# The order of the w1 side's units in the Strassen groups of a SwiGLU's first pair: its third product ahead of its fourth, and the second products spread between them

## The chip, the cores and the metric

One core of one Trainium2 chip runs the program. The metric is the device time of one execution in microseconds (us), as the median of several runs. The profile is of one further execution of the same kernel, with a time of its own.

## The reference

An FNet block (a Fourier mixing of the sequence) and a SwiGLU block, each behind a layer norm whose scale and shift come from a condition vector c. S = 2048 positions, D = 512 features, F = 1792 hidden features, all fp32. Cut to what matters:

```python
mod = (_silu(c) @ w_mod).reshape(1, 6, 1, -1)
sa, ca, ga, sb, cb, gb = (mod[:, i] for i in range(6))
h = _layernorm(x) * (1 + ca) + sa
a = einsum("bsd,ed->bse", h, dft_hid_re); b = einsum("bsd,ed->bse", h, dft_hid_im)
x = x + ga * (einsum("ts,bse->bte", dft_seq_re, a) - einsum("ts,bse->bte", dft_seq_im, b))
h = _layernorm(x) * (1 + cb) + sb
gate, up = h @ w1, h @ w3
x = x + gb * ((_silu(gate) * up) @ w2)
```

The change lies in the last two lines, the SwiGLU.

## The kernel before

**Numbers.** Every fp32 operand is held as two tiles, a high part and a low part (names ending in h and l), and every product is made of three matmuls: high by high, low by high, high by low. So w1h and w1l are the parts of a block of w1, h2h and h2l of the normed input, and hf holds both parts of the hidden tile silu(gate) * up.

**Tiling.** The sequence lies in four tiles t of 512 positions, the hidden features in seven blocks g of 256. The tiles form two pairs, (0, 2) and (1, 3). For a block and a pair, the products with w1 and with w3 are done by Strassen's scheme: seven products where eight would be due, with sums of quarters of the weight (w1s, w3s and their parts w1sh, w1sl, w3sh, w3sl) and sums of input tiles (th, tl). One such (block, pair) is a group. `items` lists twelve groups, `i` counts them: i = 0 to 4 are the blocks 2 to 6 of the first pair, i = 5 to 11 those of the second.

**Units.** A group's work on TensorE (PE) is a list of units of six matmuls each: a1 to a7 are the seven products with w1, b1 to b7 those with w3, and y is one *second product*, a piece of the product with w2 of the group before; eight of these are due in a group. The main loop at lines 1799 to 1825 has the order as a string. For i = 1 to 4 it is a head, `-b7 a1 a2 -b4 -b3` (the minus marks the last w3 units of the group before), and then `body`; i = 0 has the head `a1 a2`. Other groups have strings of their own, so `body` as the diff has it holds for i = 0 to 4 alone. Here y1 to y5 are the second products in `body`, in their order.

**PSUM banks.** The seven products of a side are accumulated in three banks (`TO`, line 1222): products 1, 6, 7 and 4 go one after the other on top of one another into the side's first bank (0 for w1, 3 for w3), product 2 into the second, products 5 and 3 into the third. Between two of them the bank's content is read out, in `factor` (lines 1361 to 1407):

- after 1, 6 and 5, ScalarE (ACT) copies the bank to a tile x or y (`copy`, L87);
- after 7, 2 and 3, VectorE (DVE) adds such a tile to the bank (`plus`, L93), into v for w1 and in place for w3;
- after 4 the bank is used itself, for w1 by the silu on ACT (L1244), for w3 by a multiplication on DVE (L96).

So a7 can't start before ACT has copied what a6 left, and a4 can't start before DVE has added what a7 left; for w3 b7 waits for the copy after b6, and b4 for the addition after b7 in the same way. a3 waits for the copy of what a5 left in its own bank, and for nothing of a7 or a4. Each y takes bank 6 or 7 in turn and is read out by ACT (L335), or by DVE in four units of i = 0 (L1153, its y2 to y5); a second product thus waits for the reading out of the second product two before. Every two of them are added to a sum in HBM by a DMA that GpSimd (POOL) issues (L1160).

**After the w3 units.** The tile v (silu(gate) times up) is copied to hf's high part on ACT one unit later and its low part is made on DVE another unit later (`behind`, `result`, L87 and L90). The y units of the next group read hf.

**Other work in the same queues.** Each engine works its own queue in order. After each unit `beside` (line 1690) puts more work on DVE and ACT, by credits: first what is in `jobs`, the splitting of the next weights (`weight_jobs`, lines 1178 to 1212: w1h, w1s, w1l, w1sh, w1sl and the same for w3, `w2h` and `w2l` for w2); and only when `jobs` is empty, the `background`: the second layer norm of tiles 1 and 3 (`ln2`, line 818: t, L826, L828, L838, L840, a square root on ACT at L880 that needs another activation table, its reciprocal L883, L847, L848, xc at L96 and L894). The jobs of the next group's w1 are queued at a3, those of its w3 at b3, those of w2 at b2.

A second kernel for other input (`general`) lies behind a branch and isn't executed.

Of the kernel before, what the change touches and what calls it, by code (L numbers as in the profile page):

```python
# [42 lines left out]
def folded(nc, pools, c, cp, wmr, wmc, x, xt, ctr, cti, wdr, wdi, w1, w3, w2, out):  # L43
# [1659 lines left out]
    def down(g, pair, *which):  # L1703
        key = which[-1]
        drain(lambda: (key, "l") in done, jobs)
        delayed()
        if (g, pair) in SEVEN:
            seven_unit(g, pair, *which)
        else:
            down_unit(g, pair, *which)  # L1710
        beside(1.36, USED["own" if pair == 1 and g >= NG - 2 else "y"])
# [85 lines left out]
    ln2(1)  # L1797
    ln2(3)
    for i in range(len(items)):
        body = "a6 a5 y a7 y y a4 y a3 y b1 y b2 y b6 b5 y"  # L1800
        if i and items[i - 1] in SEVEN:
            body = "a6 a5 a7 y a3 a4 y b1 b2 y b6 b5 y"
        spread = i > 1 and items[i - 2] in SEVEN
        if spread and i < len(items) - 1:
            body = body.replace("a6", "a6 y", 1)
        if i == len(items) - 2:
            body = "a6 y a5 y a7 a3 y a4 b1 y b2 b6 y b5"
        if i == turning:
            body = "y y y y y a6 y a5 y a7 y b1 b2 a4 b6 a3 b5"
        if i == len(items) - 1:  # L1810
            body = "a6 a5 a7 a3 a4 b1 b2 y b6 y b5 y b7 y b4 y y b3 y y y y y y y y y y"
        head = "-b7 a1 -b4 -b3 a2 " if i == turning else "-b7 a1 a2 -b4 -b3 " if i else "a1 a2 "
        if spread and i < len(items) - 1:
            head = "-b7 a1 y a2 -b4 y -b3 "
        if i == len(items) - 1:
            head = "-b7 y a1 a2 y -b4 y -b3 "
        for at in (head + body).split():
            if at == "y":
                if (i, len(seconds)) == (len(items) - 1, 4):
                    tc.mark_branch_hint_location("general", hint="LikelyTaken")  # L1820
                down(*seconds.popleft())
            elif at[0] == "-":
                unit(at[1], i - 1, int(at[2]))
            else:
                unit(at[0], i, int(at[1]))
# [710 lines left out]
def fnet_swiglu_block(  # L2536
# [26 lines left out]
    pools = consts, small, big, psum  # L2563
    args = c, cp, wmr, wmc, x, xt, ctr, cti, wdr, wdi, w1, w3, w2, out
    bad = folded(nc, (*pools, dram, tc), *args)
    flag = nc.values_load(
        bad[0:1, 0:1],
# [62 lines left out]
```

## Time and profile before

| | |
|---|---|
| median of 3 runs | 700.3 us (699.35 to 700.66) |
| profiled execution | 698.81 us, its span from first to last instruction 697.0 us |
| mean granted TensorE clock | 0.996 |
| busy PE / DVE / ACT / POOL | 97% / 84% / 65% / 19% of the span |
| groups i = 0 to 4 | about 317.5 to 475 us of the span |

The profile's page gives each engine's busy time, the granted clock in 40 slices, and the chain of work that ended last. A row of the timeline has the start in us, the busy time of one instruction or of a run of equal ones, the engine, the line, the operation, output and inputs by the program's names, and in brackets the idle time ahead of it with what ended that. Matmuls are pipelined, so the row's busy time is longer than their spacing: it is the starts of two rows that tell how far apart they were.

### The profile page before, as it was taken

How to read it: one execution, taken by the hardware profiler on the slowest of the kernel's cores; microseconds unless marked ns; L12 is line 12 of the kernel's file. 1: busy time of each engine (PE TensorE's matmuls, PEld its weight loads, DVE VectorE, ACT ScalarE, POOL GpSimd, SP SyncE). 2: the span in 40 equal slices, each digit the busy share in tenths (PEclk: the TensorE clock that was granted, in tenths of full speed). 3: DMA queues.
4: the chain of work that ended last, by engine and by line, in shares of the span. 5: the costliest groups of instructions: out<-in, count | busy, mean ns of one | idle time of the engine just before them, and what ended most of it. 6: DMA issues, size and time to landing. Idle time of an engine off the chain costs nothing.

```text
span 697.0 us, 9026 instructions
## 1 busy us (share of the span) xinstructions
PE 677.9 (97%) x3122; PEld 557.1 (80%) x3122; DVE 587.9 (84%) x945; ACT 451.4 (65%) x751; POOL 133.6 (19%) x156
## 2 busy tenths in 40 slices
PE   7999899999999999999999999999999999999996
PEld 5898778888888888888877788787877888888785
DVE  5999779987999977989987886898899979888373
ACT  4998965455343665664566767677676978777620
POOL 1320253543445000100100001011002221121100
PEclk9999999999999999999999999999999999999999
DMA  8730299787578431363758566456939898999703
GB/s 265 217 122 1 74 329 364 254 291 243 186 287 294 152 140 31 63 119 121 133 114 166 132 151 124 88 94 144 265 87 200 150 221 163 187 212 170 186 39 125
DMA packets 40261, 116.80 MB, mean 168 GB/s; under 512 B 5136, under 2 KB 5392, under 8 KB 40208
## 3 DMA queue, kind: packets, MB, share of 16 engines
q0 software_dynamic: 14512, 50.86, 35.8%
q1 hardware_dynamic: 25264, 63.98, 27.6%
q10 hardware_dynamic: 432, 1.31, 0.6%
q8 instruction: 26, 0.43, 0.3%
q14 instruction: 27, 0.22, 0.1%
HBM read 76.81 MB, written 41.42 MB: 170 GB/s over the span
## 4 chain that ended last, share of the span: by engine, by line
PE 73%; DVE 11%; ACT 8%; issue 3%; DMA 3%; SPq 1%; another core or an unknown queue 1%; POOL 0%; ACTq 0%; POOLq 0%
PE bank L100 45%; PE bank L750 25%; PE bank L559 1%; DMA wmr<-in_wmr 1%; ACT y L335 1%; DMA sum<-y 1%; ACT hf L87 1%; DVE v L96 1%; PE bank L598 1%; DVE xc L96 1%; SPq L231 1%; ACT xc L894 1%; DVE x L93 1%; DVE w3s L90 1%; DVE v L93 1%
## 5 line engine op out<-in xcount | busy, mean ns | idle before, releaser
L100 PE MATMUL bank<-hf,w2h 128*128 128x512 f32 (+1 forms) x352 | 108.8, 390 | 0.5 <-ACT y L335 0.4
L87 ACT ACTIVATE hf<-v 128x512 fp32r<-128x512 f32 x71 | 44.3, 630 | 64.6 <-DVE v L96 53.8
L335 ACT ACTIVATE y<-bank,gb 128x512 f32<-128x512 f32 x118 | 76.5, 682 | 5.2 <-PE bank L100 5.1
L100 PEld LDWEIGHTS bank<-hf,w2h 128*128 128x128 f32 x352 | 65.4, 188 | 16.9 <-ACT y L335 2.2
L1160 POOL DMA_DIRECT2D sum<-y x28 | 24.0, 857 | 245.1 <-ACT y L335 125.1
L100 PE MATMUL bank<-hf,w2l 128*128 128x512 f32 (+1 forms) x176 | 68.1, 387 | 0.0
L90 DVE TENSOR_TENSOR hf<-v,hf 128x512 fp32r<-128x512 f32 x71 | 48.8, 687 | 13.8 <-ACT hf L87 13.8
L1352 POOL DMA_DIRECT2D sum<-y x35 | 29.8, 852 | 129.3 <-ACT y L335 124.9
L750 PE MATMUL bank<-d,us 128*128 128x512 f32 x128 | 49.9, 390 | 1.0 <-DVE ho L93 1.0
L750 PE MATMUL bank<-bh,us 128*128 128x512 f32 x128 | 49.9, 390 | 0.0
L750 PE MATMUL bank<-bh,ul 128*128 128x512 f32 x128 | 49.8, 389 | 0.0
L750 PE MATMUL bank<-d,uh 128*128 128x512 f32 x128 | 49.8, 389 | 0.0
L750 PE MATMUL bank<-l,us 128*128 128x512 f32 x128 | 49.8, 389 | 0.0
L750 PE MATMUL bank<-l,uh 128*128 128x512 f32 x128 | 49.8, 389 | 0.0
L170 POOL DMA_INDIRECT re<-in_ctr,mirror x32 | 37.2, 1162 | 65.6 <-DVE ul L90 38.5
L87 ACT ACTIVATE x<-bank 128x512 f32<-128x512 f32 x72 | 41.5, 591 | 11.9 <-PE bank L100 11.8
L170 POOL DMA_INDIRECT im<-in_cti,mirror x32 | 32.8, 1025 | 36.6 <-PE bank L750 11.6
L100 PEld LDWEIGHTS bank<-hf,w2l 128*128 128x128 f32 x176 | 33.0, 188 | 6.7
L93 DVE TENSOR_TENSOR v<-bank,x 128x512 f32<-128x512 f32 x36 | 24.7, 687 | 15.9 <-PE bank L100 14.8
L1244 ACT ACTIVATE v<-v 128x512 f32<-128x512 f32 x36 | 22.7, 630 | 23.2 <-DVE v L93 22.8
L93 DVE TENSOR_TENSOR x<-bank,x 128x512 f32<-128x512 f32 x36 | 24.6, 685 | 9.4 <-PE bank L100 9.1
L100 PE MATMUL bank<-h2h,w1h 128*128 128x512 f32 x80 | 31.1, 389 | 0.0
(260 smaller groups left out, 1906.3 us busy)
## 6 DMA issues: line engine op xcount, KB each, us to landing
sum<-y POOLq DMA_DIRECT2D x63, 512.0 KB
w<-in_w SPq DMA_DIRECT2D x42, 512.0 KB
re<-in_ctr SPq DMA_DIRECT2D x32, 256.0 KB
im<-in_cti SPq DMA_DIRECT2D x32, 256.0 KB
wmc<-in_wmc SPq DMA_DIRECT2D x8, 512.0 KB
xr<-in_xt SPq DMA_DIRECT2D x8, 512.0 KB
sum<-xr SPq DMA_DIRECT2D x8, 512.0 KB
x<-in_x SPq DMA_DIRECT2D x11, 256.0 KB
```

The lines of the kernel that those rows point to most:

```text
L87: nc.scalar.activation(dst, src, AF.Copy, scale=scale)
L90: nc.vector.tensor_tensor(out=dst, in0=a, in1=b, op=OP.subtract)
L93: nc.vector.tensor_tensor(out=dst, in0=a, in1=b, op=OP.add)
L96: nc.vector.tensor_tensor(out=dst, in0=a, in1=b, op=OP.mult)
L100: nc.tensor.matmul(acc, lhs[a], rhs[b], start=first and n == 0, stop=last and n == len(PASSES) - 1, skip_group_check=more,)
L170: nc.gpsimd.indirect_dma_start(dst, None, rows, bass.IndirectOffsetOnAxis(ap=at, axis=0))
L231: queue.dma_start(raw_w[dt][q * 64 : (q + 1) * 64, m, :], w[i][par::2, q])
L335: nc.scalar.activation(dst, src, AF.Identity, scale=by)
L750: nc.tensor.matmul(acc[what, e], lhs, rhs, start=begin and i == 0, stop=(end or (turn and what == "x")) and i == len(terms) - 1, skip_grou ...
L1160: nc.gpsimd.dma_start(sums[t, d // 2], y, accum_op=OP.add)
L1244: behind(k != 0 or q == 0, lambda: nc.scalar.activation(v, src, AF.Silu))
L1352: nc.gpsimd.dma_start(sums[t, which], y, accum_op=OP.add)
```

## The change

```diff
-        body = "a6 a5 y a7 y y a4 y a3 y b1 y b2 y b6 b5 y"
+        body = "a6 a5 y y a7 y a3 y a4 y b1 y b2 y b6 b5 y"
```

y2 goes ahead of a7, and a3 and a4 change places. The units y1, y3, y4 and y5 keep their places in the list, and so do all the units behind y5. From a6 to a7 it is 4 units where it was 3, from a7 to a4 4 where it was 3, from a5 to a3 5 where it was 7. What hangs on a unit moves with it: reading out a7's and a4's bank, and the queueing of the next group's w1 jobs at a3, two units earlier than before. `beside` then fills in jobs and background at other places, so the queues of DVE and ACT change their order in more places than PE's.

ACT's queue in i = 2 at y1, before; x_3520 is the copy of what a6 left, x_3578 the copy of what a5 left, bank_531 is y1's bank and bank_535 is y2's, and L1244 on v_3522 is the silu after a7:

```order
L87 ACTIVATE hf_3559<-v_3262 128x512
L87 ACTIVATE x_3520<-bank_517_3513 128x512
L87 ACTIVATE x_3578<-bank_527_3571 128x512
L335 ACTIVATE y_3585<-bank_531_3586,gb 128x512
L87 ACTIVATE w3sh_3596<-w3s_3580 128x1024
L1244 ACTIVATE v_3522<-v_3522 128x512
L335 ACTIVATE y_3585<-bank_535_3608,gb 128x512
```

And the same place in the changed kernel, where x_3523 and x_3585 are the two copies, bank_534 is y1's and bank_536 is y2's, and v_3525 belongs to the silu after a7:

```order
L87 ACTIVATE hf_3561<-v_3262 128x512
L87 ACTIVATE x_3523<-bank_517_3516 128x512
L87 ACTIVATE x_3585<-bank_529_3578 128x512
L87 ACTIVATE w3sh_3589<-w3s_3572 128x1024
L335 ACTIVATE y_3591<-bank_534_3592,gb 128x512
L335 ACTIVATE y_3591<-bank_536_3602,gb 128x512
L1244 ACTIVATE v_3525<-v_3525 128x512
```

The reading out of y1 now stands behind w3sh, which needs DVE's sums w3s, and the silu after a7 stands behind the reading out of y2.

DVE's queue in i = 1 around the addition after a7, before; bank_474 is the bank of a1, a6, a7 and a4, v_3263 takes the addition after a7, bank_484 is the bank of a3 and v_3262 takes its addition, and t, r, q and s belong to the layer norm of a tile:

```order
L90 TENSOR_TENSOR w3l_3333<-w_448_3131,w3h_3295 128x1024
L90 TENSOR_TENSOR w3sl_3337<-w3s_3319,w3sh_3335 128x1024
L93 TENSOR_TENSOR v_3263<-bank_474_3254,x_3317 128x512
L93 TENSOR_TENSOR t_3076<-t_3076 128x512
L826 STREAM_TRANSPOSE t_3076<-t_3076 128x512
L828 TENSOR_REDUCE r_492_3358<-t_3076 128x16
L838 COPY q_494_3376<-r_492_3358 32x16 x4
L840 TENSOR_REDUCE s_494_3381<-q_494_3376 32x16
L93 TENSOR_TENSOR v_3262<-bank_484_3310,x_3261 128x512
```

And the same place in the changed kernel:

```order
L90 TENSOR_TENSOR w3l_3333<-w_447_3108,w3h_3295 128x1024
L90 TENSOR_TENSOR w3sl_3337<-w3s_3319,w3sh_3335 128x1024
L93 TENSOR_TENSOR t_3078<-t_3078 128x512
L93 TENSOR_TENSOR v_3263<-bank_474_3254,x_3317 128x512
L826 STREAM_TRANSPOSE t_3078<-t_3078 128x512
L828 TENSOR_REDUCE r_492_3357<-t_3078 128x16
L93 TENSOR_TENSOR v_3262<-bank_484_3310,x_3261 128x512
```

The addition after a7 now has one more instruction of the layer norm ahead of it, and the addition after a3 two steps fewer.

DVE's queue in i = 1 between the w1 jobs and the addition after b2, before; x_3419 with bank_507 is that addition, w1sl the last of the w1 jobs, s, w and stat belong to the layer norm:

```order
L90 TENSOR_TENSOR w1sl_3441<-w1s_3423,w1sh_3439 128x1024
L93 TENSOR_TENSOR x_3419<-bank_507_3443,x_3419 128x512
L96 TENSOR_TENSOR v_3262<-v_3262,x_3419 128x512
L90 TENSOR_TENSOR hf_3454<-v_3262,hf_3454 128x512
L90 TENSOR_TENSOR w2l_3473<-w_483_3307,w2h_3452 128x1024
L883 RECIPROCAL s_494_3381<-s_494_3381 32x16
L847 COPY w_512_3476<-s_494_3381 32x16 x4
L848 STREAM_TRANSPOSE stat_3174<-w_512_3476 128x512
```

And in the changed kernel, where x_3431 with bank_507 is that addition:

```order
L90 TENSOR_TENSOR w1sl_3406<-w1s_3380,w1sh_3397 128x1024
L838 COPY q_503_3417<-r_492_3357 32x16 x4
L840 TENSOR_REDUCE s_503_3422<-q_503_3417 32x16
L883 RECIPROCAL s_503_3422<-s_503_3422 32x16
L847 COPY w_506_3444<-s_503_3422 32x16 x4
L848 STREAM_TRANSPOSE stat_3174<-w_506_3444 128x512
L93 TENSOR_TENSOR x_3431<-bank_507_3450,x_3431 128x512
L96 TENSOR_TENSOR v_3262<-v_3262,x_3431 128x512
L90 TENSOR_TENSOR hf_3459<-v_3262,hf_3459 128x512
```

The layer norm's steps from L838 to L848 now stand ahead of the addition after b2, where its two reductions stood far ahead and L883 to L848 stood behind it.

## The prediction

> **What bounds the kernel now.** I read the page first, then the busy time in the stretch of the five groups that the change touches, and then PE's timeline there, row by row.
>
> ```profile
> span 697.0 us, 9026 instructions
> PE 677.9 (97%) x3122; PEld 557.1 (80%) x3122; DVE 587.9 (84%) x945; ACT 451.4 (65%) x751; POOL 133.6 (19%) x156
> PE 73%; DVE 11%; ACT 8%; issue 3%; DMA 3%; SPq 1%; another core or an unknown queue 1%; POOL 0%; ACTq 0%; POOLq 0%
> ```
>
> The span is 697.0 us and PE is busy for 97% of it; on the chain that ended last PE has the most. The profiled execution took 698.81 us, so 1.8 us lie around the span, and the median of the runs, 700.3 us, is 1.5 us above it. I work out a difference in the profiled execution and take it off 700.3.
>
> ```profile
> 317.50:475.00 157.50, 155.52 (x672) 124.76 (x671) 134.40 (x220) 104.91 (x154) 17.01 (x20) 1.00 0.60 130
> ```
>
> In these 157.50 us PE is busy for 155.52 and DVE, the next, for 134.40. So a gain has to come out of PE's small gaps, and DVE has 157.50 - 134.40 = 23.1 us to spare, 4.6 a group. PE's rows show where the gaps lie: the second matmul of a dependent unit starts later than its place.
>
> ```profile
> 384.29 0.39 PE L100 MATMUL bank<-hf,w2h 128*128 128x512 f32 x1
> 384.74 0.39 PE L100 MATMUL bank<-hf,w2l 128*128 128x512 f32 x1
> 384.97 0.39 PE L100 MATMUL bank<-hf,w2h 128*128 128x512 f32 x1
> 385.79 0.40 PE L100 MATMUL bank<-hf,w2l 128*128 128x512 f32 x1
> ...
> 386.67 0.50 PE L100 MATMUL bank<-th,w1sh 128*128 128x512 f32 x1 [0.49 <-ACT x L87]
> ```
>
> This is y1 and the start of a7 in i = 2. Three matmuls lie between 384.29 and 384.97, so undisturbed they are (384.97 - 384.29) / 3 = 0.227 us apart, and a unit of six takes 1.36. The row at 385.79 should stand at 384.97 + 0.454 = 385.42; it is 0.37 late. a7 should start one matmul after 385.79, at 386.02, and starts at 386.67: 0.65 late, and the row names ACT's copy as the releaser. After each such halt the next matmul is late once more by about 0.11.
>
> **The change, term by term.** PE's rows for a4 in i = 1, for a4 in i = 2, and for a7 and a4 in i = 4:
>
> ```profile
> 358.57 0.39 PE L100 MATMUL bank<-hf,w2l 128*128 128x512 f32 x1
> 359.22 0.50 PE L100 MATMUL bank<-th,w1h 128*128 128x512 f32 x1 [0.26 <-DVE v L93]
> ...
> 390.67 0.39 PE L100 MATMUL bank<-hf,w2l 128*128 128x512 f32 x1
> 391.34 0.50 PE L100 MATMUL bank<-th,w1h 128*128 128x512 f32 x1 [0.29 <-DVE v L93]
> 391.68 0.40 PE L100 MATMUL bank<-tl,w1h 128*128 128x512 f32 x1
> ...
> 447.05 0.39 PE L100 MATMUL bank<-hf,w2h 128*128 128x512 f32 x1
> ...
> 447.83 0.40 PE L100 MATMUL bank<-hf,w2l 128*128 128x512 f32 x1
> ...
> 448.72 0.50 PE L100 MATMUL bank<-th,w1sh 128*128 128x512 f32 x1 [0.49 <-ACT x L87]
> ...
> 453.39 0.50 PE L100 MATMUL bank<-th,w1h 128*128 128x512 f32 x1 [0.29 <-DVE v L93]
> 453.73 0.39 PE L100 MATMUL bank<-tl,w1h 128*128 128x512 f32 x1
> ```
>
> By the same arithmetic a4 is late by 359.22 - 358.57 - 0.227 = 0.42 in i = 1 and 0.44 in i = 2, and a7 in i = 4 by 448.72 - 447.83 - 0.227 = 0.66. y1 in i = 4 is late by 447.83 - 447.05 - 0.454 = 0.33. The halt after each can be read off the last pair: 453.73 - 453.39 - 0.227 = 0.11. a4 in i = 4 I take like that in i = 2, since its row names the same releaser with the same idle time, 0.29. With 0.11 each, the a4 halts come to 0.53 + 0.55 + 0.55 = 1.63 and the a7 halts to 0.76 + 0.77 = 1.53.
>
> The reason for each is in the queue of the engine that reads the bank:
>
> ```profile
> 357.34 1.23 DVE L90 TENSOR_TENSOR w3sl<-w3s,w3sh 128x1024 fp32r<-128x1024 f32 x1
> 358.48 0.68 DVE L93 TENSOR_TENSOR v<-bank,x 128x512 f32<-128x512 f32 x1
> 359.08 0.68 DVE L93 TENSOR_TENSOR t<-t 128x512 f32<-128x512 f32 x1
> ```
>
> In i = 1 the addition after a7 (358.48) stands behind w3sl; it ends at 359.16, and a4, due at 358.80, starts at 359.22. In the changed list two more units, a3 and y4, lie ahead of a4, so it is due at 358.80 + 2 x 1.36 = 361.52. The addition ends later by the one step t that now stands ahead of it, at about 359.8 (t's place is 0.6 long by the starts of the rows). That is 1.7 before it is wanted, so 0.53 goes. What hides the addition is the two units on PE; without them t would make the halt 0.6 longer. In i = 2 it is the same with a4 due at 390.90 + 2.72 = 393.62 and its addition done by 391.34 + 0.6. In i = 4 two steps h2l stand ahead of the addition, each like this row:
>
> ```profile
> 453.25 1.22 DVE L90 TENSOR_TENSOR h2l<-xc,h2h 128x1024 fp32r<-128x1024 f32 x1
> ```
>
> With 2 x 1.22 more it ends at 453.33 + 2.44 = 455.8 at the worst, while a4 is due at 452.94 + 2.72 = 455.66; but w3s start some 3.5 us earlier there (third rival), so I count 0.55 for it, and 0 as the bound against it.
>
> ```profile
> 382.63 0.82 ACT L894 ACTIVATE xc<-xc,sb,cb 128x512 f32<-128x512 f32 x1 [0.50 <-DVE xc L96]
> 384.58 1.04 ACT L87 ACTIVATE w3h<-w 128x1024 fp32r<-128x1024 f32 x1
> 386.05 0.57 ACT L87 ACTIVATE x<-bank 128x512 f32<-128x512 f32 x1
> 387.00 0.68 ACT L335 ACTIVATE y<-bank,gb 128x512 f32<-128x512 f32 x1
> ```
>
> In i = 2 the copy after a6 starts at 386.05 and ends at 386.62, and a7 starts at 386.67. Ahead of the copy ACT had L894 twice (382.63, 0.82), hf, w3h (1.04) and hf. In the changed list y2 lies ahead of a7, so a7 is due at 386.02 + 1.36 = 387.38 (387.01 if y1's halt goes): with the old queue the copy is done 0.4 to 0.8 before that, and the changed queue has L894 of this tile further ahead, in i = 1. What could undo it is a later w3h or hf; there are 0.4 of cover. a7's term goes in i = 2, and in i = 4, whose rows read alike: 1.53. y1's 0.37 in i = 2 goes for the most part with L894; I count 0.3 of it. y1 in i = 4 keeps its own, since there hf's low part now stands behind the four sums w3s.
>
> The w3 side in i = 1 and, for b7, in i = 3:
>
> ```profile
> 374.08 0.39 PE L100 MATMUL bank<-hf,w2l 128*128 128x512 f32 x1
> 374.42 0.50 PE L100 MATMUL bank<-th,w3sh 128*128 128x512 f32 x1
> ...
> 378.41 0.39 PE L100 MATMUL bank<-h2h,w1l 128*128 128x512 f32 x1
> 378.71 0.50 PE L100 MATMUL bank<-th,w3h 128*128 128x512 f32 x1
> ...
> 436.13 0.39 PE L100 MATMUL bank<-hf,w2l 128*128 128x512 f32 x1
> 436.47 0.50 PE L100 MATMUL bank<-th,w3sh 128*128 128x512 f32 x1
> ```
>
> b7 is late by 0.11 + 0.11 in i = 1 and by as much in i = 3; b4 by 0.07 + 0.11 in i = 1, and I take the same for i = 3. In i = 1 and 3 together 0.8. They have their cause in the addition after b2, which waits for the w1 jobs; these are queued two units (2.7 us) earlier now. What takes that place is the layer norm, which the change puts ahead of the addition after b2:
>
> ```profile
> 362.98 1.28 ACT L880 ACT_TABLE_LOAD   x1
> 364.27 0.31 ACT L880 ACTIVATE s<-s,eps 32x16 f32<-32x16 f32 x1
> ...
> 375.09 0.23 DVE L883 RECIPROCAL s<-s 32x16 f32<-32x16 f32 x1
> ...
> 376.09 0.71 DVE L848 STREAM_TRANSPOSE stat<-w 128x512 f32<-128x512 f32 x1
> ```
>
> The square root takes 1.28 + 0.31 with its table, and DVE from L883 to the end of L848 376.80 - 375.09 = 1.71. In the changed queue the root stands behind the copy after b1. b7 is due at 374.08 + 0.227 = 374.31, b1 starts seven units before, at 364.79, so in the changed kernel, 0.53 earlier by a4's halt, b1 ends at 365.6. Then follow, with 0.2 until PE's last row ends, the copy (0.57), the root (1.59), L883 to L848 (1.71), the addition and the product after b2 (0.6 + 0.7): 371.0. On ACT hf (taken as a copy), y7's reading out (as at 387.00), w2h (as w3h) and at last the copy after b6 follow, 0.57 + 0.68 + 1.04 + 0.57 = 2.86 by their busy times and about 2.6 as they overlap: 373.6 to 373.9, where b7 is due at 374.31 - 0.53 = 373.78. That is no margin, so of the 0.4 in i = 1 I count 0.2. In i = 3 the root stands ahead of the copy, 0.6 earlier: 0.4.
>
> In i = 0 the halts are short, and their rows are left out: y4's (0.2) goes because y2 is read out earlier, and L838 and L840 now stand ahead of the addition after b2, which makes b7 later by about as much or a little more: -0.1, between +0.2 and -0.3. In i = 4 the b side can lose: w1sl needs a tile that y1 and y2 give back when their sum has landed.
>
> ```profile
> 330.25 0.85 POOL L1160 DMA_DIRECT2D sum<-y  x1 [29.23 <-DVE y L1153]
> ...
> 338.58 0.85 POOL L1160 DMA_DIRECT2D sum<-y  x1 [4.32 <-DMA sum<-y]
> ```
>
> The sum issued at 330.25 had landed at 338.58, when the issue waiting for it began: 8.3 us. In i = 4 that sum is issued behind y2's reading out, by the rows above at about 451, lands at about 459.5 and holds w1sl until then; the addition after b2 stands behind it, so b7 loses 0 to 0.6 (half a w1sl); I count 0.3.
>
> The sum: a4 1.63, a7 1.53, y1 0.3, w3 side of i = 1 and 3 0.6, i = 0 -0.1, b7 in i = 4 -0.3: 3.66, say **3.7 us**, for 698.81 - 3.7 = 695.1 in the profiled execution and 700.3 - 3.7 = **696.6** on the median. With all the unsure terms against me (no a4 in i = 4, nothing from y1, 0.2 from the w3 side, i = 0 and i = 4 as bad as they may be) it is 1.08 + 1.53 + 0.2 - 0.3 - 0.6 = 1.9, with all for me 1.63 + 1.53 + 0.37 + 0.8 + 0.2 = 4.5. PE's later groups have the same order in both kernels, so what is won is kept.
>
> [...] The row at 362.98 takes 1.28, and the activation follows at 364.27, 0.01 after its end. [...]
>
> **Rivals.** (1) *The halts move.* The bank is read out earlier, but the queues that read it are the same, and a halt won at a7 comes back at y3 or b7. Against it: 23.1 us of DVE's time are free. Then a4's 1.63 remain, 1.0 to 2.2 with some of the rest: about 698.7.
>
> (2) *DVE or ACT sets the group's pace* and every microsecond that PE wins in a group is waited for at b7 and b4, as it is already in i = 1 and i = 3: no change, 700.3. For it: these halts at b7 although DVE's queue was filled in good order. Against it: the 4.6 us a group.
>
> (3) *Slower, by w3sh ahead of y1's reading out.* y3 takes the bank that y1 leaves, and y1's reading out on ACT now stands behind w3sh in i = 2, 3 and 4, which waits for w3s:
>
> ```profile
> 450.41 1.06 ACT L87 ACTIVATE w3sh<-w3s 128x1024 fp32r<-128x1024 f32 x1 [0.69 <-DVE w3s L90]
> ```
>
> In i = 4 before, w3s were ready at 450.4, and ACT had waited 0.69 for them. Were they as late in the changed kernel, y1's reading out there would end behind w3sh, a copy and h2h (1.06 + 0.57 + 1.04 and 0.68 for itself, h2h taken as w3h) at 453.8, where y3 is due three units after y1, at 447.05 - 0.68 + 3 x 1.36 = 450.45: 3.3 lost. In i = 2, which by the rows of a7 runs 448.72 - 386.67 = 62.05 earlier, without the copy and h2h, it would be 388.36 + 1.06 + 0.68 = 390.1 against 384.29 + 4.08 = 388.37: 1.7, and in i = 3 the same. 6.7 against 3.7 won: 3.0 slower, 703.3. In the changed queue w3s stand ahead of hf's low part and behind no xc, by my count 3.5 earlier in i = 4 and 2.6 in i = 2. So it decides from where they come 0.2 later than that in i = 4, and 0.9 in i = 2; a small halt at y3 of i = 4 is likely enough, all three are not.
>
> [...]
>
> **Chances.** The forecast 0.60 (695.8 to 698.4), the first rival 0.18 (698.1 to 699.3), no change 0.12, slower 0.08, the table 0.02. The range holds the forecast and the first and fourth rivals, with 0.6 below for the spread of the runs (699.35 to 700.66): 695.2 to 699.4. 0.2% or 1.4 us is about what a measurement of this kernel can tell from no change. Faster by more: 0.60, 0.13 of the first rival and 0.02, 0.75 together. Within: 0.05 and 0.12, 0.17. Slower: 0.08.
>
> **What would show it.** Right: in i = 1, 2 and 4 a4 starts 0.23 after the matmul ahead of it, and a7 too in i = 2 and 4; PE's busy time in the stretch hardly changes while the stretch gets 3.7 shorter; y1 in i = 4 still halts by 0.3. [...]

## The result, and the profile after

The changed kernel is faster: 695.43 us against 699.83 (medians of six runs each), ratio 0.9941 with a 95% interval from 0.9928 to 0.9954. By the ratio that is 4.1 us, between 3.2 and 5.0; the two medians lie 4.4 apart. A second measurement beside other kernels (e7 below) gave 0.9946, from 0.9933 to 0.9959. Forecast were 696.6 and a gain of 3.7.

The profiled execution took 694.86 us. From its page, the span, the busy time of the engines and the chain that ended last:

```profile
span 693.1 us, 9032 instructions
PE 675.3 (97%) x3122; PEld 558.1 (81%) x3122; DVE 586.9 (85%) x945; ACT 451.1 (65%) x751; POOL 131.6 (19%) x156
PE 71%; DVE 9%; issue 7%; DMA 5%; ACT 4%; POOL 1%; SPq 1%; another core or an unknown queue 1%; POOLq 0%; ACTq 0%; DVEq 0%
```

PE is still at 97%, with the same 3122 matmuls; its busy time fell by 2.6 us, less than the span, and the rest was idle time. To see where the time went, the span is cut at matmuls that both kernels have. The first mark is the first matmul of a1 of i = 0. The second is the fourth matmul of a2 of i = 5, which stands behind b7, b4 and b3 of i = 4, so all units of the five groups lie between the two. These are their rows in PE's timeline, of before and then of after:

```profile
317.47 0.39 PE L100 MATMUL bank<-h2h,w1h 128*128 128x512 f32 x1
...
474.65 0.39 PE L100 MATMUL bank<-h2h,w1h 128*128 128x512 f32 x1
```

```profile
318.00 0.39 PE L100 MATMUL bank<-h2h,w1h 128*128 128x512 f32 x1
...
470.82 0.39 PE L100 MATMUL bank<-h2h,w1h 128*128 128x512 f32 x1
```

The groups took 474.65 - 317.47 = 157.18 us and take 470.82 - 318.00 = 152.82: **4.36 less**. The first row stands 0.53 later after: ahead of it both kernels have the same instructions, and one execution differs from the next there by more than that (last section). From the second row to the last matmul it is 215.4 and 215.6, and from there to the end of the span 7.0 and 6.7. So all of the gain arose in the five groups, and what they won was kept.

The rows that answer to those of before, PE at a4 in i = 1 and at a7 in i = 2 and 4, each with the matmul ahead of it:

```profile
361.94 0.39 PE L100 MATMUL bank<-hf,w2l 128*128 128x512 f32 x1
362.17 0.39 PE L100 MATMUL bank<-th,w1h 128*128 128x512 f32 x1
...
386.70 0.39 PE L100 MATMUL bank<-hf,w2l 128*128 128x512 f32 x1
386.93 0.40 PE L100 MATMUL bank<-th,w1sh 128*128 128x512 f32 x1
...
446.80 0.39 PE L100 MATMUL bank<-hf,w2l 128*128 128x512 f32 x1
447.02 0.39 PE L100 MATMUL bank<-th,w1sh 128*128 128x512 f32 x1
```

All three follow at 0.22 to 0.23, the undisturbed distance; there is no halt at any a7 or a4 of the five groups. What is left are b7 in i = 0, b7 in i = 1 and y1 in i = 4:

```profile
343.61 0.39 PE L100 MATMUL bank<-hf,w2l 128*128 128x512 f32 x1
344.36 0.50 PE L100 MATMUL bank<-th,w3sh 128*128 128x512 f32 x1 [0.36 <-ACT x L87]
...
374.18 0.39 PE L100 MATMUL bank<-hf,w2l 128*128 128x512 f32 x1
374.50 0.50 PE L100 MATMUL bank<-th,w3sh 128*128 128x512 f32 x1
...
444.74 0.39 PE L100 MATMUL bank<-hf,w2h 128*128 128x512 f32 x1
...
445.42 0.40 PE L100 MATMUL bank<-hf,w2l 128*128 128x512 f32 x1
```

These are 0.52, 0.09 and 0.23 late, 1.05 in all with 0.1 behind each of the first two, where before had 5.1.

### The profile page after: what moved, and what is told of

Read it like the earlier page. It is cut to its first block, busy times and chain, and to the rows that moved or that the text cites. A ratio compares the mean times of both kernels' runs of the same rounds, so it can differ in the third digit from the quotient of the medians.

```text
span 693.1 us, 9032 instructions
## 1 busy us (share of the span) xinstructions
PE 675.3 (97%) x3122; PEld 558.1 (81%) x3122; DVE 586.9 (85%) x945; ACT 451.1 (65%) x751; POOL 131.6 (19%) x156
## 3 DMA queue, kind: packets, MB, share of 16 engines
q10 hardware_dynamic: 432, 1.31, 0.5%
## 4 chain that ended last, share of the span: by engine, by line
PE 71%; DVE 9%; issue 7%; DMA 5%; ACT 4%; POOL 1%; SPq 1%; another core or an unknown queue 1%; POOLq 0%; ACTq 0%; DVEq 0%
PE bank L100 43%; PE bank L750 25%; DMA sum<-y 3%; POOL sum L1352 1%; PE bank L559 1%; DMA w<-in_wdr 1%; PE bank L598 1%; ACT y L335 1%; DVE v L96 1%; SPq L231 1%; DMA w<-in_wdi 1%; DVE xr L805 1%; DVE ul L90 1%; DMA x<-in_x 0%
## 5 line engine op out<-in xcount | busy, mean ns | idle before, releaser
L170 POOL DMA_INDIRECT re<-in_ctr,mirror x32 | 35.1, 1095 | 64.8 <-DVE ul L90 38.5
L1244 ACT ACTIVATE v<-v 128x512 f32<-128x512 f32 x36 | 22.7, 629 | 22.5 <-DVE v L93 22.1
```

Of the source, the lines that this page charges most:

```text
L170: nc.gpsimd.indirect_dma_start(dst, None, rows, bass.IndirectOffsetOnAxis(ap=at, axis=0))
L1244: behind(k != 0 or q == 0, lambda: nc.scalar.activation(v, src, AF.Silu))
```

## The experiments

Two theories of what removed the halts at a7 and a4 were put against each other. **S, spacing:** the units that now lie between two products on the same bank cover the reading out of that bank. **Q, queue:** a3 now comes earlier and queues the next group's w1 jobs earlier, so that other work on ACT and DVE (the layer norm's L894 and t) falls into another place and no longer stands ahead of that reading out. The changed kernel does both at once. The table has all kernels that ran, worked out from each trace like the 157.18 above, before rounding: the time up to a1 of i = 0 (ahead), the five groups, from there to the last matmul's start (behind), and from that to the end of the span (end). Each ratio is to the kernel before on the same chip.

| kernel | ahead | groups | behind | end | ratio to before, 95% interval |
|---|---|---|---|---|---|
| before | 317.5 | 157.18 | 215.4 | 7.0 | |
| after; again (e7) | 318.0; 316.0 | 152.83; 152.83 | 215.6; 216.7 | 6.7; 6.9 | 0.9941 (0.9928 to 0.9954); 0.9946 (0.9933 to 0.9959) |
| e1: a3 and a4 swapped only | 318.5 | 153.55 | 215.4 | 8.8 | 0.9976 (0.9965 to 0.9987) |
| e5: e1, SyncE's code moved | 316.1 | 153.61 | 216.8 | 6.9 | 0.9958 (0.9940 to 0.9975) |
| e2: y2 moved only | 318.8 | 164.26 | 215.4 | 9.2 | 1.0132 (1.0115 to 1.0148) |
| e9: e2, jobs early, SyncE's code moved | 316.7 | 157.22 | 215.4 | 6.9 | 0.9983 (0.9972 to 0.9994) |
| e3: after, jobs late | 318.0 | 154.37 | 215.3 | 9.0 | 0.9980 (0.9966 to 0.9993) |
| e11: e3, SyncE's code moved | 318.6 | 154.43 | 215.8 | 7.0 | 0.9955 (0.9939 to 0.9970) |
| e4: before, jobs early | 320.9 | 153.79 | 215.9 | 8.7 | 0.9990 (0.9978 to 1.0001) |
| e6: e4, SyncE's code moved | 316.8 | 153.77 | 215.3 | 7.3 | 0.9952 (0.9939 to 0.9965) |
| e10: e5, a7 right behind a5 | 315.9 | 158.39 | 215.6 | 6.7 | 1.0014 (1.0003 to 1.0025) |
| e8: b6 ahead of y7 | 316.8 | 152.39 | 215.8 | 7.0 | 0.9936 (0.9922 to 0.9951) |

The groups repeat to 0.07 us wherever the same groups ran twice, so this column separates kernels that the time alone does not.

**e1, only a3 and a4 change places.**

```diff
-        body = "a6 a5 y a7 y y a4 y a3 y b1 y b2 y b6 b5 y"
+        body = "a6 a5 y a7 y y a3 y a4 y b1 y b2 y b6 b5 y"
```

> Only a3 and a4 change places; y2 stays behind a7, three units from a6 to a7. Theory S (spacing: each halt went because units were put between the two products that share a bank): a4's halts go (1.63), a7's in i = 2 and 4 stay (1.53), so 2.2 to 2.8 us faster than before. Rival Q (queue: a7's halts went because a3 now queues the w1 jobs two units earlier, so that the layer norm's L894 runs in i = 1 and 3 and no longer ahead of the copy after a6): a7's halts go here too, and 3.8 to 4.4 us are won, all of the change.

The groups won 3.63 of 4.35, and a7's halts, which S expected to stay, are gone but for 0.21 in i = 2; a new one of 0.42 arose at y4 in i = 1. On a7 Q is right, though the groups won a little less than its 3.8. But the kernel won only 1.7 us (0.9 to 2.5), less than either theory said. The table shows where the rest was lost: 1.8 us more between the last matmul and the end.

**e2, only y2 moves.**

```diff
+        body = "a6 a5 y y a7 y a4 y a3 y b1 y b2 y b6 b5 y"
```

> Only y2 goes ahead of a7; a4 and a3 as before, so two units from a7 to a4 and the w1 jobs queued where they were. Theory S: a7's halts go (1.53). But a4 waits for DVE's addition, which stands behind w3l and w3sl and comes when it came before, so what is won at a7 in i = 2 and 4 is waited for at a4 (halts of 1.2 to 1.4 there): 0 to 0.4 us faster than before, the same by the measurement. Rival Q: a7's halts stay and a4's grow by nothing: no change either, but with a7's rows still 0.65 late.

Both theories said next to no change; it is 9.2 us slower. a7's halts did go, with the old queue, as S said and Q did not, but a4 lost far more than S had counted. PE and then DVE around a4 in i = 2 of e2, with a4's row in i = 4 at the end of PE's rows:

```profile
392.42 0.39 PE L100 MATMUL bank<-hf,w2l 128*128 128x512 f32 x1
394.96 0.63 PE L100 MATMUL bank<-th,w1h 128*128 128x512 f32 x1 [2.15 <-DVE v L93]
395.38 0.63 PE L100 MATMUL bank<-tl,w1h 128*128 128x512 f32 x1
...
460.45 0.80 PE L100 MATMUL bank<-th,w1h 128*128 128x512 f32 x1 [2.58 <-DVE v L93]
```

```profile
391.94 1.23 DVE L90 TENSOR_TENSOR w3sl<-w3s,w3sh 128x1024 fp32r<-128x1024 f32 x1
393.08 1.22 DVE L93 TENSOR_TENSOR t<-xr,xr 128x1024 f32<-128x1024 f32 x1
394.22 0.68 DVE L93 TENSOR_TENSOR v<-bank,x 128x512 f32<-128x512 f32 x1
```

The addition after a7 (394.22) stands behind w3sl and now also behind the layer norm's first t of 1.22, which fell one place earlier; a4 is 394.96 - 392.42 - 0.227 = 2.31 late. And then six matmuls follow at 0.43 instead of 0.23: PE runs at half its clock, as the windows of this stretch say in the third column from the right:

```profile
394.00:396.00 2.00, 1.04 (x3) 0.85 (x4) 1.97 (x4) 1.06 (x2) 0.00 (x0) 0.79 0.98 137
396.00:398.00 2.00, 2.00 (x7) 1.52 (x6) 1.84 (x7) 0.39 (x2) 0.00 (x0) 0.50 0.65 129
398.00:400.00 2.00, 2.00 (x9) 1.67 (x8) 0.00 (x0) 0.77 (x2) 0.00 (x0) 0.85 0.00 0
```

A clock of 0.79, 0.50 and 0.85 in these 6 us is 0.5 for 0.84 + 2.00 + 0.60 = 3.4 us. The same happens in i = 4 (the row at 460.45, with 2.58 of idle time): the granted clock is 0.51 and 0.64 in the two stretches of 2 us from 460 on, 3.4 us at 0.5 again, with matmuls 0.43 apart from 461.04 to 463.18. There an h2l of 1.23, which waited 0.29 for ACT, has come ahead of the addition; in i = 0, where a4 halts by 1.55, it is a t again. So the place of this side work decides a4, as Q claims of the queues, in a direction that neither theory had seen.

**e3, the changed order with the jobs late.**

```diff
-        if (kind, n) == ("a", 7 if i == turning else 3) and more:
+        if (kind, n) == ("a", 7 if i == turning else 4 if i < turning else 3) and more:
```

> The changed order of units, with the load of w3 and the w1 jobs of the next group queued at a4 instead of a3, that is at the place in the list where they were queued before. Theory S: a7's and a4's halts are gone as in the changed kernel, and only the earlier jobs' own share comes back (y1 in i = 2 0.3, b7 and b4 in i = 1 and 3 0.6): 2.9 to 3.5 us faster than before. Rival Q: a7's 1.53 come back too: 1.5 to 2.2 us faster.

The groups won 2.81, just under the 2.9 to 3.5 that S expects and well over Q's 1.5 to 2.2. ACT and PE in i = 2 of e3:

```profile
383.14 0.82 ACT L894 ACTIVATE xc<-xc,sb,cb 128x512 f32<-128x512 f32 x1 [0.50 <-DVE xc L96]
...
386.56 0.58 ACT L87 ACTIVATE x<-bank 128x512 f32<-128x512 f32 x1
```

```profile
387.69 0.39 PE L100 MATMUL bank<-hf,w2l 128*128 128x512 f32 x1
387.92 0.40 PE L100 MATMUL bank<-th,w1sh 128*128 128x512 f32 x1
```

L894 is back ahead of the copy after a6, as in before, and the copy comes as late as there; a7 starts 0.23 after the matmul ahead of it all the same, because y2 lies between. What came back is y1 in i = 2 (0.37) and b7 and b4 in i = 1 and 3 (0.95 and 0.44). Time: 1.4 us won (0.5 to 2.4), under both theories' ranges, again with a long end.

**e4, the old order with the jobs early.** The edit of e3, made in the kernel before, so that the jobs are queued at a4, where the changed list has a3.

> The order of units as before, with the load of w3 and the w1 jobs queued at a4, two units earlier than before and at the place where the changed kernel queues them. Theory S: a7's and a4's halts stay, only y1's in i = 2 and some of b7's and b4's go: 0 to 0.9 us faster than before. Rival Q: a7's halts in i = 2 and 4 go: 1.5 to 2.5 us faster.

The groups won 3.39, more than the new order with the old queue. ACT and PE at a6, a7 and a4 of i = 2, in the second run of these groups (e6):

```profile
375.72 0.82 ACT L894 ACTIVATE xc<-xc,sb,cb 128x512 f32<-128x512 f32 x1 [0.88 <-DVE xc L96]
...
384.33 0.58 ACT L87 ACTIVATE x<-bank 128x512 f32<-128x512 f32 x1
```

```profile
384.62 0.39 PE L100 MATMUL bank<-hf,w2l 128*128 128x512 f32 x1
384.96 0.50 PE L100 MATMUL bank<-th,w1sh 128*128 128x512 f32 x1
...
388.99 0.39 PE L100 MATMUL bank<-hf,w2l 128*128 128x512 f32 x1
389.21 0.44 PE L100 MATMUL bank<-th,w1h 128*128 128x512 f32 x1
```

All four L894 of the tile run in one go from 375.72 (0.82 each), in i = 1's last units, and none is left ahead of the copy after a6, which comes at 384.33; a7, three units after a6 as in before, is late by 0.11 and a4 not. In i = 1 a4 keeps 0.44 of its 0.52. The measured time showed almost none of it, 0.7 us (-0.1 to 1.5): by the time alone S would have been right, and only the trace tells that a7's halts went and that the end got longer.

**e5, e6 and e11, SyncE's code moved.** What e1, e2, e3 and e4 have in common is the long end. Their pages count one more fetch of program (queue q14, an instruction queue) than before and after do, 28 against 27. SyncE, which issues the stores of the result, ends the program with a row of semaphore instructions, and in these four traces that row stops once for 1.8 to 2.3 us, ahead of the second of them in e4, the third in e2 and the sixth in e1 and e3, with a fetch of q14 in the stop; before and after have no such stop. So ten copies of a load were put into the kernel that isn't executed (`general`), which move SyncE's last instructions within its program and change nothing that runs:

```diff
+        nc.sync.dma_start(sc_row[0][:, 0, :], c.broadcast_to([P, D]))
```

> The kernel in which only a3 and a4 change places, with ten copies of one small load added to the second kernel that is never executed, so that SyncE's instructions after the last branch lie elsewhere in its program. Theory F (fetch: e1 and e4 lost 2 us of what their groups won because SyncE has to fetch one more piece of program in its last instructions): from the last row of DVE to the end of the span 5.9 to 6.2 us where e1 has 8.0, the groups as in e1, and 1.6 to 2.4 us faster than e1, 3.2 to 4.2 faster than before. Rival N (it is chance, or another chip): 8.0 again and the time of e1.

> The order of units as before with the w1 jobs queued two units earlier, as e4, and the same ten loads that are never executed. Theory F: the end 2 us shorter than in e4, the groups as in e4 (3.4 shorter than before), so 2.4 to 3.6 us faster than before, that is most of what the change brings without moving one unit. Rival N: as e4, 0.7 us faster than before.

> The changed order with the w1 jobs queued where they were before, as e3, and the ten loads that are never executed. It completes the table of order and jobs without the 2 us of the last fetch. Theory F: the end as in the changed kernel, the groups as in e3 (2.8 shorter than before), 2.0 to 3.6 us faster than before and 0.8 to 2.2 slower than the changed kernel. Rival N: as e3, 1.4 faster than before.

DVE's last row, the span and the line of q14, of e1 and of e5:

```profile
span 696.3 us, 9023 instructions
q14 instruction: 28, 0.23, 0.1%
...
687.78 0.48 DVE L1146 SCALAR_TENSOR_TENSOR xr<-bank,gb,xr 128x256 f32<-128x256 f32 x1 [0.23 <-PE bank L100]
```

```profile
span 693.3 us, 9023 instructions
q14 instruction: 27, 0.22, 0.1%
...
686.79 0.48 DVE L1146 SCALAR_TENSOR_TENSOR xr<-bank,gb,xr 128x256 f32<-128x256 f32 x1 [0.23 <-PE bank L100]
```

From the end of DVE's last row to the end of the span it is 696.3 - 688.26 = 8.0 in e1 and 693.3 - 687.27 = 6.0 in e5. All three kernels got back about the end of before (6.9, 7.3 and 7.0 us), their groups stayed, and their times are 2.9 (1.7 to 4.2), 3.4 (2.4 to 4.3) and 3.2 us (2.1 to 4.3) below before's. Theory F is right about the end. e5's 2.9 lies just under the 3.2 to 4.2 that it gave, and e5 is 1.3 us faster than e1 by the two ratios where 1.6 to 2.4 was expected. The padded kernels ran on other chips than e1 to e4; that this is not the chips' doing rests on the ratios, each to before on its own chip, and on q14's count. The gains of the groups now show in the times: early jobs alone bring 3.4 of the 4.35 in the groups, the new order alone 2.8, both together 4.35. They remove the same halts; either is enough for most of them. The edit for early jobs moves the load of w3 with them, and the two were not tried apart.

**e7** is the changed kernel again, on one chip with e5, e6 and e8.

> The changed kernel once more, beside the others on one chip. All theories: 4.1 us faster than before, between 3.2 and 5.0.

Ratio 0.9946, 3.8 us.

**e9, e2 with the jobs early** (and SyncE's code moved).

> The order of e2 (only y2 goes ahead of a7, two units from a7 to a4), but with the w1 jobs queued two units earlier, as in the changed kernel, and the ten loads that are never executed, as in e5. Theory Q2 (what made e2 slow is the layer norm's step t that DVE's queue had ahead of the addition after a7, and PE's half clock after a halt of over 2 us; the place in the list of the w1 jobs sets that): a4 halts by 0.4 in i = 1 and by 0.1 to 0.5 in i = 0, 2, 3 and 4, no half clock, 2.0 to 3.5 us faster than before. Theory S2 (two units from a7 to a4 are too few whatever the queues do): a4 halts by over 1 us in i = 0, 2 and 4, and the kernel is slower than before by 2 us or more.

a4 halts by 1.55, 0.72, 0.92, 0.50 and 1.18 in i = 0 to 4: more than Q2 said, and over 1 us in i = 0 and 4, nearly so in i = 2, as S2 said. No halt is followed by the half clock (behind each, one matmul comes after 0.34 and those after it 0.22 to 0.24 apart), and 7.0 us of e2's loss in the groups are gone. But the groups take as long as before (157.22), and the time is 1.2 us below before's (0.4 to 2.0): neither Q2's 2.0 to 3.5 faster nor S2's 2 slower. In the two traces that 1.2 shows in no part but the one ahead of the groups (0.8 shorter), and its cause stays open. So with one unit between a7 and a4 even the queue with early jobs, in which a t of 0.69 stands ahead of the addition in i = 2, does not hide it: spacing counts too.

**e10, a7 nearer.**

```diff
+        body = "a6 a5 a7 y y y a3 y a4 y b1 y b2 y b6 b5 y"
```

> As e5 (a3 ahead of a4, never executed loads), but a7 right behind a5, two units from a6 to a7 instead of three, and y2 and y3 behind it. Theory S: a7's halts grow by the unit taken away, less what reserve there was: by 1.36 in i = 2, where e5 still has 0.22, and by 0.3 to 1.3 in i = 0, 1, 3 and 4; 2 to 5 us slower than e5. Theory Q: ACT's copy after a6 is done early once the w1 jobs are queued early, so only i = 2 halts, by 1.0 to 1.6: 1 to 2 us slower than e5.

Against e5 the groups lose 4.8 us and the kernel 3.9 (ratios 1.0014 and 0.9958). PE at a7 in i = 2 and at y3 in i = 4:

```profile
385.06 0.50 PE L100 MATMUL bank<-th,w1sh 128*128 128x512 f32 x1 [1.31 <-ACT x L87]
...
451.66 0.50 PE L100 MATMUL bank<-hf,w2h 128*128 128x512 f32 x1 [1.19 <-ACT y L335]
```

a7 is late by 1.21, 0.89, 1.59, 0.21 and 0.27 in i = 0 to 4, the 0.1 behind each counted in: S's bounds in i = 0, 1 and 2, just under them in i = 3 and 4. In i = 2, where e5 had 0.22, it is the unit taken away, 1.36. And y3, now two units behind y1, waits in i = 4 for y1's reading out, which on ACT stands behind w3sh, two h2h and now also the silu after a7: 1.35 (with 0.12 more behind it). That is the halt that the third rival of the prediction named, in a kernel that gives it room.

**e8, a better version.** b6 goes ahead of y7, four units instead of three from b6 to b7, in the changed kernel:

```diff
-        body = "a6 a5 y y a7 y a3 y a4 y b1 y b2 y b6 b5 y"
+        body = "a6 a5 y y a7 y a3 y a4 y b1 y b2 b6 y b5 y"
```

> The changed order with b6 ahead of y7, so four units instead of three from b6 to b7. Theory S (spacing): the halts at b7 that the changed kernel still has in i = 0 and 1 (0.62 and 0.20) go, nothing else changes: 0.5 to 0.9 us faster than the changed kernel. Rival Q (queue): b7 waits for ACT's copy after b6, which stands behind hf's high part and so behind the addition after b2, and that comes when it came before; the halt goes all the same only if that chain ends before b7 is due one unit later. A rival that loses: y7 now comes after b6, its sum is issued a unit later and the tiles come free later: 0 to 0.5 slower.

b7's halts go (0.82 to 0.06), 0.25 of small ones appears at y1 and b4, and the groups take 152.39, 0.44 less. Its median was 693.64 against 694.26 of the changed kernel on the same chip, the fastest of all that ran; the intervals of the two overlap, so that it is faster than the changed kernel is shown for the groups, not by the time.

## Why the prediction was right, point by point

- **a4, 1.63 forecast, 1.63 found.** The step of the queue is right to the tenth. DVE in i = 1 of the changed kernel:

```profile
359.14 0.68 DVE L93 TENSOR_TENSOR t<-t 128x512 f32<-128x512 f32 x1
359.74 0.68 DVE L93 TENSOR_TENSOR v<-bank,x 128x512 f32<-128x512 f32 x1
```

The addition stands behind t, ends at 360.42, and a4 starts at 362.17: 1.75 of cover where 1.7 was worked out. But the two units are not the only reason: in e6, without them, the early jobs leave under 0.1 of a4's halts in i = 2 and in i = 4, and only i = 1 keeps 0.44.

- **a7, 1.53 forecast, 1.53 found.** But the reason was only one of two. The prediction named y2's 1.36 as the cover and the earlier L894 as an extra; e6 shows that the extra alone takes away 1.3 of the 1.5, and e3 that the unit alone takes all.
- **y1, 0.3 forecast, 0.47 found:** 0.37 in i = 2 is gone, and y1 in i = 4 fell from 0.33 to 0.23. e3 and e4 show that this comes from the jobs alone.
- **The w3 side, 0.6 forecast, 0.6 found.** In i = 3 both halts are gone, in i = 1 half of 0.40. ACT's root and DVE's L883 in i = 1:

```profile
367.11 1.28 ACT L880 ACT_TABLE_LOAD   x1
368.41 0.31 ACT L880 ACTIVATE s<-s,eps 32x16 f32<-32x16 f32 x1
```

```profile
368.75 0.24 DVE L883 RECIPROCAL s<-s 32x16 f32<-32x16 f32 x1 [1.61 <-ACT s L880]
```

The root follows its table by 0.02 and L883 starts 0.34 after the root did; ahead of the load, which starts at 367.11, ACT's row ends at 367.10. The chance of 0.02 for the table, and the fourth rival that the range holds, stand for a wait behind the table load that no run shows: from the load's end to the root it was 0.01 in before and 0.02 here.

- **i = 0, -0.1 forecast, -0.15 found** (0.47 of halts before, 0.62 after, all at b7).
- **b7 in i = 4, -0.3 forecast, nothing found.** This is the term that was wrong. w1sl was to be held by the tile that y1's and y2's sum gives back:

```profile
455.02 1.22 DVE L90 TENSOR_TENSOR w1l<-w,w1h 128x1024 fp32r<-128x1024 f32 x1
456.29 1.23 DVE L90 TENSOR_TENSOR w1sl<-w1s,w1sh 128x1024 fp32r<-128x1024 f32 x1
```

w1sl starts as soon as w1l ends; the tile was free. The sum of y1 and y2 is issued at 449.34 here, and in the trace its packets are through at 454.4, 5.0 us after the issue and ahead of w1sl's turn. The 8.3 us of i = 0 were too long a measure: there two sums were on their way at once, issued at 330.25 and 333.42, and their packets ran side by side until 338.3.

- **The rivals.** The halts did not move to y3: in i = 4 y1's reading out, behind w3sh, starts at 446.84 and ends at 447.52, and y3 starts at 448.38:

```profile
446.84 0.68 ACT L335 ACTIVATE y<-bank,gb 128x512 f32<-128x512 f32 x1
```

```profile
448.38 0.39 PE L100 MATMUL bank<-hf,w2h 128*128 128x512 f32 x1
```

That leaves 0.86 where the prediction had 0.2 to spare. DVE did not become the bound: it is busy for 133.0 of the groups' 152.8 us.
- **A sign that did not hold.** PE's busy time in the stretch was to change hardly. In the groups it fell from 155.20 to 152.46 us, by 2.74 of the 4.36. A row's 0.39 reaches 0.16 beyond the 0.227 to the next start, so the first 0.16 of a halt counts as busy (a4 in i = 2 was 0.44 late, with 0.29 of idle time in its row), and the late matmul itself counts 0.50. Busy time thus hides part of each halt; the starts of the rows don't.

The terms found come to 1.63 + 1.53 + 0.47 + 0.6 - 0.15 = 4.1, the groups to 4.36; the rest lies in delays of under 0.05 each.

## What to carry to other kernels

When code that queues side work hangs on a unit, moving that unit moves two things, the dependent work on TensorE and the order of every in-order queue beside it; test the two apart before crediting either, since here each alone removed most of the halts. A move that only counts distances can lose far more than it could win (e2), if it puts one long step ahead of the instruction that TensorE waits for. And compare pieces of the trace between common instructions: kernels whose totals differed by 2 us had the same groups and another end.

## What the runs showed of the hardware that was not expected

- **Half clock after halts of 2.15 and 2.58 us.** In e2 PE idled 2.15 us in i = 2 and 2.58 in i = 4, and both times the clock was at 0.5 for 3.4 us from about the end of the halt on, with matmuls 0.43 apart. The idle times of 1.31 and 1.19 us in e10 had no such effect: one matmul behind each comes after 0.33 to 0.34, those after it 0.22 to 0.24 apart, and the mean granted clock of that execution is 0.999. Whether it is the length of the halt that counts, and where between 1.31 and 2.15 a bound would lie, no run shows.
- **The end changes with where SyncE's code lies.** With one more fetch of program on q14 (28 in e1, 27 in e5) the end takes 1.3 to 2.0 us more (the end column, e1 to e5, e3 to e11 and e4 to e6), with nothing else changed that runs. Why the one place takes a fetch more than the other is not shown. A wait with fetches in it stands in the shorter ends too: 2.7 us lie between SyncE's last branch and its next instruction (692.13 to 694.79 in before, 688.16 to 690.84 in after), with two fetches of q14 in between. What e1 shows in addition is a second stop of 2.1 us, a few instructions later.
- **The part ahead of the groups varies** from 315.9 to 320.9 us between executions with the same instructions, partly by the clock granted in the first 50 us, e4's and e7's windows:

```profile
0.00:50.00 50.00, 42.77 (x262) 36.40 (x263) 38.55 (x92) 37.05 (x72) 13.13 (x28) 0.93 0.68 211
```

```profile
0.00:50.00 50.00, 43.90 (x283) 37.06 (x284) 40.91 (x98) 39.77 (x76) 13.14 (x28) 1.00 0.69 211
```

The granted clock is 0.93 in e4 and 1.00 in e7. That is not all of it: e3's clock is 1.00 there too, and its part ahead is 318.0 where e7's is 316.0. The part behind varies as well, from 215.3 to 216.8. A single profile of this kernel can therefore not be compared by its total.
